# Linear attention and spectral mixing on one core: attention numerators of both head halves in one 128-row product

## The chip, the cores and the metric

The kernel runs on one core of a Trainium2 chip. The metric is the device time of one execution in microseconds, and lower is better. Data lie in HBM. SBUF is the on-chip memory with 128 partitions, and PSUM holds matmul results. TensorE (PE in the profile) multiplies; PEld is its loading of the stationary operand. VectorE (DVE), ScalarE (ACT), GpSimd (POOL) and SyncE (SP) are the other engines. Each engine works through its own instructions in order. POOL and SP here do little but issue DMA transfers, and POOL's transfers convert float32 in HBM to 16 bits in SBUF.

## The reference

There are two layers in a row. The first is linear attention over 8 batches, 8 heads, 576 rows and a head dimension of 64:

```python
def phi(x):
    return np.where(x > 0, x, np.exp(x) - 1.0) + 1.0
q_p, k_p = (phi(q), phi(k))
kv = np.einsum('bhsd,bhse->bhde', k_p, v)
z = np.sum(k_p, axis=2)
num = np.einsum('bhsd,bhde->bhse', q_p, kv)
den = np.einsum('bhsd,bhd->bhs', q_p, z)[..., None] + 1e-06
x = num / den
```

Its output, with the heads side by side, is x of 576 rows and 512 columns per batch. The second layer takes the real FFT along the rows, multiplies the first 64 modes with complex 512 x 512 matrices (one pair of matrices, `w_r` and `w_i`, per mode), leaves the other modes zero, transforms back to y, and gives `u + max(u @ w_ch, 0)` with `u = x + y`. The weights of the modes are 134 MB in float32, most of what the kernel reads.

## The kernel before

**Attention stage.** One loop runs over the 8 batches. `load` brings q, k and v of the batch two ahead, in two buffers each. `exps` (ACT) and `features` (DVE) form phi of q and k; `features` also copies v into `vpad`, which has one buffer and carries a column of ones, so that the sum z comes out of the same products as kv. In each turn of the loop the work is given in this order: `turn_q` transposes phi of q (PE, line 236) and copies it to SBUF (ACT, line 243); `sum_kv` sums kv of the batch (PE, line 256) and copies the parts that belong to one head to `kv_all` (ACT, line 268); `features` of the next batch; `exps` of the batch after next; then `form_x` five times, each for a set of rows. `form_x` multiplies transposed q with kv (`num_matmuls`, line 162), takes the reciprocal of the denominators (DVE, line 289) and multiplies (DVE, line 292) to get x in float16. Between these stand the forward DFT of the batch before (`transform`, line 354) and `place_x` (lines 322 to 343), which lays out the spectra of the batch before that for the mode products.

The order on each engine is written out by hand: `pin` keeps an instruction in program order. Three slots of PSUM (tag `big`) go round among the transposes, kv sums, numerators and spectra, in the order in which these are given.

A head pair fills the 128 partitions, so a batch has kv in four blocks of two 64-row halves. `num_matmuls` makes one matmul of 64 rows and 65 columns for each half (64 numerators and the denominator): eight per row set.

**Weights.** The modes go in pairs. The first five pairs are loaded during the attention stage, two into `wpool` and three into a pool that is given up afterwards. Every further pair reuses a buffer of `wpool`, so its load (POOL, line 116) waits until the product that used the buffer is done. On POOL's queue the loads of these first five pairs are followed by `wch16`, the channel weights (line 513), and `pick_sb` (line 515), and then by the sixth pair.

**Weight stage.** For each pair, `mode_pair` makes 16 matmuls (line 431), evacuates the result (lines 446 and 448), and transposes and sums it with `pick_sb` (line 454). Two slots per pair, "mid" and "end", take other work off a list: first `attention_rows`, which computes the numerators again for each of the 36 row tiles, this time as float32 rows of the final x (lines 162, 620 and 622); the constant row sets (`row_sets`, `row_set`), which stand after the eighth tile in the list; then the inverse DFT of the lower modes with the first channel products (lines 655 to 686), and the products that the last modes need. The denominators of even batches are kept from the attention stage, those of odd batches are taken again.

**Tail.** After the last weights have landed, the rest of the inverse DFT and of the channel product is added for pairs of row tiles (lines 737 to 810) and the rows are stored.

Of the kernel before, what the change touches and what calls it, by code (L numbers as in the profile page):

```python
# [10 lines left out]
F32 = mybir.dt.float32  # L11
F16 = mybir.dt.float16
# [31 lines left out]
def kernel(  # L44
# [10 lines left out]
    nc = tc.nc  # L55

    B, H, S, Dh = q.shape
    D = H * Dh
    NM = moe_w_r.shape[0]
    NHP = H // 2  # L60
    NDC = D // 128
# [15 lines left out]
    const = ctx.enter_context(tc.tile_pool(name="const", bufs=1, side="right"))  # L77
# [3 lines left out]
    id16 = const.tile([128, 128], F16, name="id16")  # L81
    fwd_sb = const.tile([128, 5, 2 * NM], F16, name="fwd_sb")
    pick_sb = const.tile([128, 32], F16, name="pick_sb")
    wch16 = const.tile([128, NDC, D], F16, name="wch16")
    actwarm = const.tile([128, 1], F32, name="actwarm")
    nc.vector.memset(actwarm, 0.0)
    nc.scalar.activation(out=actwarm, in_=actwarm, func=AF.Exp)
# [13 lines left out]
    kv_all = [xpool.tile([128, 2, 2, 65], F16, tag="kv", bufs=B, name=f"kv{b}") for b in range(B)]  # L101
    rd_all = [xpool.tile([128, 5, 2, 4], F32, tag="rd", bufs=B, name=f"rd{b}") for b in range(B)]

    W_KEEP = 2
    pin = tc.keep_in_program_order
    PIECES = (slice(0, 4), slice(4, 6), slice(6, 7), slice(7, 8))
    HALVES = [slice(0, 64), slice(64, 128)]
# [3 lines left out]
    def w_load(p: int, half: int, pool, tag: str, bufs: int):  # L111
        if half == 0:
            w_in[p] = pool.tile([128, NDW, D], BF16, tag=tag, bufs=bufs, name=f"w{p}")
        two = (moe_w_r, moe_w_i)[half][2 * p : 2 * p + 2]
        pin(
            nc.gpsimd.dma_start(  # L116
                out=w_in[p][half::2], in_=two.rearrange("g (r dc) e -> (g r) dc e", dc=NDW)
            )
        )
# [25 lines left out]
    def w_next():  # L145
        p, half = pending.pop(0)
        pool, tag, bufs = (wpool, "w", W_KEEP) if p < n_keep else (wpre, "wp", W_PRE)
        w_load(p, half, pool, tag, bufs)

    def rows_of(jj: int, base: int = 0):  # L150

        if jj < NJJ:
            return slice(base + jj, base + 512, NJJ)
        return slice(512, S) if base == 0 else slice(0, base)

    def num_matmuls(num, orow, qT, kv_sb, cols, pinned=False):
        for hpp in range(2):
            for h2 in range(2):
                for hpo in range(2):
                    rows = slice(hpo * 64, hpo * 64 + 64)  # L160
                    c0 = (hpp * 2 + h2) * 65
                    mm = nc.tensor.matmul(  # L162
                        num[hpo][orow, c0 : c0 + 65], qT[rows, hpp, h2, cols], kv_sb[rows, hpp, h2, :]
                    )
                    if pinned:
                        pin(mm)
        return [n[orow, 0:260].rearrange("p (c n) -> p c n", c=4) for n in num]

    def q_view(t):
        return t.rearrange("p (c t s) -> p c t s", c=2, t=2)  # L170

    qT_all = [q_tile(f"qT{b}") for b in range(B)]
# [75 lines left out]
    def sum_kv(b):  # L248

        for pair in range(2):  # L250
            kv_ps = psA.tile([128, 2, 512], F32, tag="big", bufs=3, name=f"kvp{b}_{pair}")
            for j in range(2 * NJ):
                for h2 in range(2):
                    r0 = 64 * pair + 32 * h2
                    pin(
                        nc.tensor.matmul(  # L256
                            kv_ps[:, h2, 0:130],
                            phi["k", b][r0 : r0 + 32, j // NJ, j % NJ].rearrange("p o d -> p (o d)"),
                            vp[r0 : r0 + 32, :, j, 0:65],
                            start=(j == 0),  # L260
                            stop=(j == 2 * NJ - 1),
                            tile_position=(r0, 0),
                        )
                    )
            for hpo in range(2):
                rows = HALVES[hpo]
                pin(
                    nc.scalar.copy(
                        out=kv_all[b][rows, pair], in_=kv_ps[rows, :, hpo * 65 : hpo * 65 + 65]
                    )  # L270
                )

    def form_x(b, jj):
        if jj == 0:
            x16s[b] = (
                sA.tile([128, 2 * NJ * Dh * 2], F16, tag="x16", bufs=2, name=f"x16_{b}")[
                    :, 0 : NJJ * D
                ].rearrange("p (j d) -> p j d", j=NJJ),
                sA.tile([128, D], F16, tag="x16t", bufs=2, name=f"x16t_{b}"),
            )  # L280
        tail = jj == NJJ
        orow = HALVES[b % 2] if tail else slice(0, 128)
        num = psA.tile([128, 2, 512], F32, tag="big", bufs=3, name=f"num{b}_{jj}")
        num_matmuls(
            [num[:, o] for o in range(2)], orow, q_view(qT_all[b]), kv_all[b], rows_of(jj), True
        )
        nv = num[orow, :, 0:260].rearrange("p o (c n) -> p o c n", c=4)
        rden = rd_all[b][orow, jj]
        pin(nc.vector.reciprocal(out=rden, in_=nv[:, :, :, 64]))
        dst = x16s[b][1][orow, :] if tail else x16s[b][0][:, jj, :]  # L290
        pin(
            nc.vector.tensor_tensor(  # L292
                out=dst.rearrange("p (o c d) -> p o c d", o=2, c=4),
                in0=nv[:, :, :, 0:64],
                in1=rden.unsqueeze(3).broadcast_to([64 if tail else 128, 2, 4, Dh]),
                op=ALU.mult,
            )
        )

    place = sA.tile([128, 4, 66], BF16, name="place")  # L300
    place_l = sA.tile([128, 2, 130], BF16, name="place_l")
    nc.vector.memset(place, 0.0)
    nc.vector.memset(place_l, 0.0)

# [204 lines left out]

    while pending:  # L510
        w_next()
    tc.keep_in_program_order(
        nc.gpsimd.dma_start(out=wch16, in_=moe_w_ch.rearrange("(c p) j -> p c j", p=128))
    )
# [34 lines left out]
    sW = ctx.enter_context(tc.tile_pool(name="sW", bufs=1))  # L549
# [8 lines left out]
    BASE = (0, 64)  # L558
    out_rows = out.rearrange("b s d -> (b s) d")

    def x_of(t: int):
        if t < B * NJJ:
            return x_main[t // NJJ][:, t % NJJ, :]
        i = t - B * NJJ
        return x_tail[i // 2][:, i % 2, :]
# [10 lines left out]
    def bank(name: str, shape=(128, D), dtype=F32):  # L576
        return psB.tile(list(shape), dtype, tag="bank", bufs=4, name=name)
# [25 lines left out]
    def parts_of(t: int):  # L603
        if t < B * NJJ:
            b, jj = divmod(t, NJJ)
            return [(b, jj, slice(0, 128))]
        p = t - B * NJJ
        return [(2 * p + h, NJJ, HALVES[h]) for h in range(2)]

    def attention_rows(t: int):  # L610

        num = [bank(f"nw{t}_{o}") for o in range(2)]
        x = x_of(t)
        for b, jj, orow in parts_of(t):
            nv = num_matmuls(num, orow, q_view(qT_all[b]), kv_all[b], rows_of(jj, BASE[b % 2]), True)
            for o in range(2):
                rden = rd_all[b][orow, jj, o]
                if b % 2 == 1:
                    rden = sW.tile([128, 4], F32, tag="rdw", bufs=4, name=f"rdw{t}_{o}")[orow]
                    pin(nc.vector.reciprocal(out=rden, in_=nv[o][:, :, 64]))  # L620
                pin(
                    nc.vector.tensor_tensor(  # L622
                        out=x[orow, o * 256 : o * 256 + 256].rearrange("p (c d) -> p c d", c=4),
                        in0=nv[o][:, :, 0:64],
                        in1=rden.unsqueeze(2).broadcast_to([orow.stop - orow.start, 4, Dh]),
                        op=ALU.mult,
                    )
                )

    def early_rows(b: int):  # L630

# [56 lines left out]
    tiles = []  # L688
# [63 lines left out]
    for b in range(B):  # L752
        pairs += [(b * NJJ, b * NJJ + 1), (b * NJJ + 2, b * NJJ + 3)]
        if b % 4 == 3:
            k = b // 4
# [90 lines left out]
    def share(n_items: int, steps: list):  # L846
        total, at = sum(w for _, w in steps), 0
        for key, w in steps:
            lo = at
            at += w  # L850
            slots[key] = slots.get(key, 0) + n_items * at // total - n_items * lo // total
# [13 lines left out]
    def first_rows(n: int):  # L865
# [7 lines left out]
            )  # L873

    rows_work = [row_sets] + [lambda i=i: row_set(i) for i in range(1 + N_LEAD)]
    work[:0] = [lambda t=t: attention_rows(t) for t in tiles[:8]] + rows_work + [
        lambda t=t: attention_rows(t) for t in tiles[8:]
    ]
    share(
        len(tiles) + len(rows_work),  # L880
        [((p, h), 1) for p in range(n_early, first_fold) for h in ("mid", "end")],
# [22 lines left out]
    rows = [Y8[:, ec].rearrange("p m n -> p (m n)") for ec in range(NDC)]  # L904
# [17 lines left out]
    for h, eng in enumerate((nc.sync, nc.gpsimd)):  # L922
        eng.dma_start(
            out=YZ_all[64 * h : 64 * h + 64 : NF // NL].rearrange("r b z d -> r b (z d)"),
            in_=last.rearrange("p z d -> p (z d)"),
# [10 lines left out]
    def add_one(n: int, i: int):  # L936
# [8 lines left out]
            out=x_of(0), in0=accs[0][:, 0], scalar=0.0, in1=x_of(0), op0=ALU.max, op1=ALU.add  # L945
# [51 lines left out]
```

## Time and profile before

| | |
|---|---|
| Median of 3 runs | 421.31 us (421.26 to 423.99) |
| Profiled execution | 421.64 us, span 419.9 us |
| PE busy | 289.4 us (69%) |
| PEld busy | 156.2 us (37%) |
| DVE busy | 228.3 us (54%) |
| ACT busy | 153.7 us (37%) |
| POOL busy | 57.0 us (14%) |
| Mean granted TensorE clock | 0.79 |
| HBM read, written | 163.9 MB, 9.4 MB |

The span is the time from the first to the last instruction in the profiler's record; the execution's own time has a little around it. Busy shares are averages over stages that differ: the attention stage (to about 113 us), the weight stage (to about 384 us) and the tail. In lines of the timeline the first two columns are the start and the duration in microseconds; then come the engine, the line of the kernel, the operation, its output and inputs with their shapes, how many instructions are merged, and in brackets the idle time of the engine just before, with what ended it. The granted clock of TensorE is a share of its full speed.

### The profile page before, as it was taken

What the parts mean: (1) busy time and instruction counts of PE and PEld (TensorE: products, weight loads), DVE (VectorE), ACT (ScalarE), POOL (GpSimd) and SP (SyncE); (2) the same over time, 40 slices, a digit from 0 to 9 for tenths busy, and PEclk for the clock granted to TensorE, in tenths of its full rate; (3) what the DMA queues carried; (4) which work ended last, traced back from release to release, by engine and by line L of the source; (5) the groups of instructions that cost most, each with busy time, mean ns of one, the idle gap of its engine ahead of it and who ended that gap; (6) DMA issues with size and microseconds to landing.
All of it is one profiled execution on the core that took longest, in us unless ns stands there. A gap on an engine that the chain in (4) does not pass through costs nothing.

```text
span 419.9 us, 7345 instructions
## 1 busy us (share of the span) xinstructions
PE 289.4 (69%) x3094; PEld 156.2 (37%) x3094; DVE 228.3 (54%) x495; ACT 153.7 (37%) x253; POOL 57.0 (14%) x99
## 2 busy tenths in 40 slices
PE   0359998999617553444343686979787978999992
PEld 0247776877301221222121232424333423364420
DVE  3588899695404462464645353455544533422794
ACT  4677797854201011000000233334342532230782
POOL 4222224210001111111111111101111111130000
PEclk9999988599855555555555589898998988899997
DMA  8999999999999999999999999999999999997698
GB/s 217 211 212 217 210 222 205 229 204 223 219 220 212 213 223 211 215 223 207 220 220 208 222 220 209 220 219 208 221 222 208 219 219 211 220 209 158 237 390 326
DMA packets 16417, 93.17 MB, mean 222 GB/s; under 512 B 2032, under 2 KB 2944, under 8 KB 11968
## 3 DMA queue, kind: packets, MB, share of 16 engines
q0 software_dynamic: 12416, 81.48, 93.2%
q1 hardware_dynamic: 3968, 11.22, 7.2%
q8 instruction: 24, 0.39, 0.3%
q14 instruction: 9, 0.07, 0.0%
HBM read 163.93 MB, written 9.44 MB: 413 GB/s over the span
## 4 chain that ended last, share of the span: by engine, by line
DMA 62%; PE 24%; DVE 5%; issue 3%; ACT 3%; POOL 2%; DVEq 0%; ACTq 0%; POOLq 0%
DMA w<-in_moe_w_i_dram 49%; DMA pick_sb<-row_pick 8%; PE P L431 8%; DMA k<-in_k_dram 5%; PE acc L737 3%; PE acc L776 2%; PE kvp L256 2%; PE zl L418 2%; POOL w L116 2%; PE eps L678 2%; ACT ke L207 1%; DVE x L292 1%; PE yt L454 1%; ACT ys L448 1%; DVE ke L220 1%
## 5 line engine op out<-in xcount | busy, mean ns | idle before, releaser
L431 PE MATMUL P<-w,xz 128*32 128x512 bf16 x496 | 49.4, 538 | 65.1 <-DMA w<-in_moe_w_i_dram 62.6
L448 ACT CAST ys<-P 128x512 f16<-128x512 f32 x15 | 8.8, 585 | 127.9 <-PE P L431 127.9
L116 POOL DMA_DIRECT2D w<-in_moe_w_r_dram x31 | 17.4, 560 | 246.3 <-PE P L431 241.8
L431 PEld LDWEIGHTS <-xz 128*32 128x32 bf16 x496 | 13.4, 116 | 86.8 <-DMA w<-in_moe_w_i_dram 55.4
L446 DVE CAST ys<-P 128x512 f16<-128x512 f32 x17 | 11.8, 692 | 56.8 <-PE P L431 56.8
L678 PE MATMUL eps<-wch,xTw 128*128 128x512 f16 x144 | 40.9, 412 | 0.0
L162 PEld LDWEIGHTS <-qT 64*128 64x128 f16 (+1 forms) x640 | 23.4, 124 | 31.3 <-issue 17.5
L661 ACT CAST x16w<-x_main 128x512 f16<-128x512 f32 x32 | 19.8, 618 | 37.0 <-DVE x_main L659 37.0
L659 DVE TENSOR_TENSOR x_main<-ya,x_main 128x512 f32<-128x512 f32 x32 | 22.0, 690 | 20.8 <-PE ya L655 20.5
L256 PE MATMUL kvp<-vpad,ke 32*128 32x130 f16 x576 | 24.6, 261 | 9.0 <-ACT qT L243 6.2
L686 ACT CAST E<-eps 128x512 f16<-128x512 f32 (+1 forms) x40 | 21.2, 539 | 22.6 <-PE eps L678 22.6
L441 DVE COPY xz<-xt_c 64x256 bf16<-64x256 bf16 x62 | 23.1, 372 | 11.2 <-PE P L431 10.4
L256 PEld LDWEIGHTS <-ke 32*128 32x128 f16 x576 | 22.4, 115 | 10.8 <-issue 8.3
L162 PE MATMUL nw<-kv,qT 64*128 64x65 f16 (+1 forms) x320 | 18.9, 240 | 9.5 <-DVE x_tail L622 4.5
L292 DVE TENSOR_TENSOR x<-num,rd 128x512 f16<-128x512 f32 x32 | 22.1, 691 | 1.1
L236 PE MATMUL qTp<-id,qe 128*128 128x128 f16 x144 | 13.3, 265 | 11.2 <-DVE qe L220 9.7
L207 ACT ACTIVATE qe<-q 128x1152 f16<-128x1152 f16 (+1 forms) x16 | 17.9, 1157 | 8.0 <-DMA q<-in_q_dram 7.9
L622 DVE TENSOR_TENSOR x_main<-nw,rd 128x256 f32<-128x256 f32 x32 | 11.2, 415 | 17.3 <-PE nw L162 17.3
L162 PE MATMUL num<-kv,qT 64*128 64x65 f16 (+1 forms) x320 | 16.6, 219 | 5.1 <-DVE x L292 2.4
L243 ACT COPY qT<-qTp 128x1152 f16<-128x1152 f16 x16 | 19.6, 1292 | 0.7 <-PE qTp L236 0.6
L454 PE MATMUL yt<-pick_sb,ys 128*128 128x32 f16 (+1 forms) x128 | 8.7, 185 | 16.0 <-DMA pick_sb<-row_pick 9.8
L207 ACT ACTIVATE ke<-k 128x1152 f16<-128x1152 f16 x16 | 17.7, 1154 | 5.3 <-DMA k<-in_k_dram 3.9
(117 smaller groups left out, 492.5 us busy)
## 6 DMA issues: line engine op xcount, KB each, us to landing
w<-in_moe_w_r_dram POOLq DMA_DIRECT2D x31, 1024.0 KB, 12.5
w<-in_moe_w_i_dram POOLq DMA_DIRECT2D x31, 1024.0 KB, 16.9
out_dram<-x_main SPq DMA_DIRECT2D x10, 512.0 KB, 4.7
k<-in_k_dram POOLq DMA_DIRECT2D x8, 576.0 KB, 12.9
v<-in_v_dram POOLq DMA_DIRECT2D x8, 576.0 KB, 14.4
q<-in_q_dram POOLq DMA_DIRECT2D x7, 576.0 KB, 12.6
out_dram<-x_main SPq DMA_DIRECT2D x2, 1024.0 KB, 4.9
q<-in_q_dram SPq DMA_DIRECT2D x2, 576.0 KB, 4.6
```

Source lines behind the costliest of these rows:

```text
L116: nc.gpsimd.dma_start(out=w_in[p][half::2], in_=two.rearrange("g (r dc) e -> (g r) dc e", dc=NDW))
L162: mm = nc.tensor.matmul(num[hpo][orow, c0 : c0 + 65], qT[rows, hpp, h2, cols], kv_sb[rows, hpp, h2, :])
L207: pin(nc.scalar.activation(out=ev[:, c], in_=heads(nm, b, c), func=AF.Exp))
L243: nc.scalar.copy(out=qT[:, :, c * NJ : (c + 1) * NJ], in_=qT_ps.rearrange("p j x -> p x j"))
L256: nc.tensor.matmul(kv_ps[:, h2, 0:130], phi["k", b][r0 : r0 + 32, j // NJ, j % NJ].rearrange("p o d -> p (o d)"), vp[r0 : r0 + 32, :, j, 0 ...
L292: nc.vector.tensor_tensor(out=dst.rearrange("p (o c d) -> p o c d", o=2, c=4), in0=nv[:, :, :, 0:64], in1=rden.unsqueeze(3).broadcast_to([ ...
L431: nc.tensor.matmul(P[c : c + n, :], x, w[:, dc, :], start=(dc < NDC), stop=(dc >= n_dc - NDC), tile_position=(0, c), skip_group_check=True,)
L441: pin(nc.vector.tensor_copy(out=xz[p % 2][HALVES[h], :, h, :], in_=src))
L659: pin(nc.vector.tensor_tensor(out=x, in0=acc, in1=x, op=ALU.add))
L661: pin(nc.scalar.copy(out=x16w[t], in_=x))
L678: nc.tensor.matmul(e_ps, xT[:, c, :], wch16[:, c, :], start=(c == 0), stop=(c == NDC - 1))
L686: pin(nc.scalar.copy(out=dst, in_=e_ps[:, cols]))
```

## The change

The two halves of a head pair become one matmul. Its moving operand is a block-diagonal kv: 128 rows and 2 x 65 columns, with the first head's kv in the upper rows and left columns, the second head's in the lower rows and right columns, and zeros elsewhere. A row set then takes four matmuls of 128 rows and 130 columns instead of eight of 64 rows and 65 columns, and its result lies in PSUM in a different order of columns.

In the attention stage the block-diagonal tile `bd_all` has space for two batches. It lies in the space that the channel weights take later: both have the tag `wch` with one buffer, so `wch16` is now allocated after the loop. `sum_kv` lets ACT copy into `bd_all`, and two new copies on VectorE at its end fill `kv_all` from it. In the weight stage a second such tile, `kv_diag_w`, is filled from `kv_all` by `set_kv`, one row tile ahead of its use. It takes the space (tag `rows`) in which the row sets' selector and later `ye_slots` lie, so the row sets now come after all attention rows.

```diff
-    wch16 = const.tile([128, NDC, D], F16, name="wch16")
+    bd_all = const.tile([128, NDC * D], F16, tag="wch", bufs=1, name="kv_diag")[:, 0 : 2 * 520]
+    bd_all = bd_all.rearrange("p (i a h n) -> p i a h n", i=2, a=2, h=2)
...
-    def num_matmuls(num, orow, qT, kv_sb, cols, pinned=False):
+    def num_matmuls(num, orow, qT, kv_bd, cols):
         for hpp in range(2):
             for h2 in range(2):
-                for hpo in range(2):
-                    rows = slice(hpo * 64, hpo * 64 + 64)
-                    c0 = (hpp * 2 + h2) * 65
-                    mm = nc.tensor.matmul(
-                        num[hpo][orow, c0 : c0 + 65], qT[rows, hpp, h2, cols], kv_sb[rows, hpp, h2, :]
-                    )
-                    if pinned:
-                        pin(mm)
-        return [n[orow, 0:260].rearrange("p (c n) -> p c n", c=4) for n in num]
+                c0 = h2 * 256
+                pin(nc.tensor.matmul(num[hpp][orow, c0 : c0 + 130], qT[:, hpp, h2, cols], kv_bd[:, hpp, h2]))
+
+    def diag_part(kv_bd, hpo: int):
+
+        return kv_bd[HALVES[hpo], :, :, hpo * 65 : hpo * 65 + 65]
...
                 pin(
                     nc.scalar.copy(
-                        out=kv_all[b][rows, pair], in_=kv_ps[rows, :, hpo * 65 : hpo * 65 + 65]
+                        out=diag_part(bd_all[:, b % 2], hpo)[:, pair],
+                        in_=kv_ps[rows, :, hpo * 65 : hpo * 65 + 65],
                     )
                 )
+        for hpo in range(2):
+            pin(nc.vector.tensor_copy(out=kv_all[b][HALVES[hpo]], in_=diag_part(bd_all[:, b % 2], hpo)))
...
+    nc.vector.memset(bd_all, 0.0)
     nc.vector.memset(place, 0.0)
...
     while pending:
         w_next()
+    wch16 = const.tile([128, NDC, D], F16, tag="wch", bufs=1, name="wch16")
     tc.keep_in_program_order(
         nc.gpsimd.dma_start(out=wch16, in_=moe_w_ch.rearrange("(c p) j -> p c j", p=128))
     )
...
+    bdw: list = []
+
+    def set_kv(b: int):
+
+        if not bdw:
+            bdw.append(sW.tile([128, 2, 2, 2, 130], F16, tag="rows", bufs=1, name="kv_diag_w"))
+            nc.vector.memset(bdw[0], 0.0)
+        for hpo in range(2):
+            pin(nc.vector.tensor_copy(out=diag_part(bdw[0][:, b % 2], hpo), in_=kv_all[b][HALVES[hpo]]))
...
+        k = tiles.index(t) + 1
+        for b in sorted({p[0] for t_next in tiles[k : k + 1] for p in parts_of(t_next)} - kv_set):
+            kv_set.add(b)
+            set_kv(b)
...
-    work[:0] = [lambda t=t: attention_rows(t) for t in tiles[:8]] + rows_work + [
-        lambda t=t: attention_rows(t) for t in tiles[8:]
-    ]
+    kv_set = {0}
+    set_kv(0)
+    work[:0] = [lambda t=t: attention_rows(t) for t in tiles] + rows_work
```

The rest of the diff follows from this: `form_x` and `attention_rows` read PSUM in its new order of columns, with as many DVE instructions of as many elements as before.

More of the change, by code (lines that the diff above doesn't have):

```diff
@@ L283, in form_x @@
         num = psA.tile([128, 2, 512], F32, tag="big", bufs=3, name=f"num{b}_{jj}")
[L284 to L288, printed above, removed]
+        num_matmuls([num[:, a] for a in range(2)], orow, q_view(qT_all[b]), bd_all[:, b % 2], rows_of(jj))
+        nv = num.rearrange("p a (h m) -> p (a h) m", h=2)[orow, :, 0:130]
+        nv = nv.rearrange("p c (o n) -> p c o n", o=2)
+        rden = rd_all[b][orow, jj].rearrange("p a (h o) -> p (a h) o", h=2)
         pin(nc.vector.reciprocal(out=rden, in_=nv[:, :, :, 64]))
@@ L292, in form_x @@
             nc.vector.tensor_tensor(
-                out=dst.rearrange("p (o c d) -> p o c d", o=2, c=4),
+                out=dst.rearrange("p (o c d) -> p c o d", o=2, c=4),
                 in0=nv[:, :, :, 0:64],
-                in1=rden.unsqueeze(3).broadcast_to([64 if tail else 128, 2, 4, Dh]),
+                in1=rden.unsqueeze(3).broadcast_to([64 if tail else 128, 4, 2, Dh]),
                 op=ALU.mult,
@@ L608, in parts_of @@
         return [(2 * p + h, NJJ, HALVES[h]) for h in range(2)]
+    bdw: list = []
[5 more added lines that the diff above has]
+            pin(nc.vector.tensor_copy(out=diag_part(bdw[0][:, b % 2], hpo), in_=kv_all[b][HALVES[hpo]]))
     def attention_rows(t: int):
-        num = [bank(f"nw{t}_{o}") for o in range(2)]
+        num = [bank(f"nw{t}_{a}") for a in range(2)]
         x = x_of(t)
         for b, jj, orow in parts_of(t):
-            nv = num_matmuls(num, orow, q_view(qT_all[b]), kv_all[b], rows_of(jj, BASE[b % 2]), True)
-            for o in range(2):
-                rden = rd_all[b][orow, jj, o]
+            num_matmuls(num, orow, q_view(qT_all[b]), bdw[0][:, b % 2], rows_of(jj, BASE[b % 2]))
+            for a in range(2):
+                nv = num[a].rearrange("p (h m) -> p h m", h=2)[orow, :, 0:130]
+                nv = nv.rearrange("p h (o n) -> p h o n", o=2)
+                rden = rd_all[b][orow, jj, a].rearrange("p (h o) -> p h o", h=2)
                 if b % 2 == 1:
-                    rden = sW.tile([128, 4], F32, tag="rdw", bufs=4, name=f"rdw{t}_{o}")[orow]
-                    pin(nc.vector.reciprocal(out=rden, in_=nv[o][:, :, 64]))
+                    rden = sW.tile([128, 2, 2], F32, tag="rdw", bufs=4, name=f"rdw{t}_{a}")[orow]
+                    pin(nc.vector.reciprocal(out=rden, in_=nv[:, :, :, 64]))
+                xv = x[orow, :].rearrange("p (o a h d) -> p a h o d", o=2, a=2, h=2)[:, a]
                 pin(
                     nc.vector.tensor_tensor(
-                        out=x[orow, o * 256 : o * 256 + 256].rearrange("p (c d) -> p c d", c=4),
-                        in0=nv[o][:, :, 0:64],
-                        in1=rden.unsqueeze(2).broadcast_to([orow.stop - orow.start, 4, Dh]),
+                        out=xv,
+                        in0=nv[:, :, :, 0:64],
+                        in1=rden.unsqueeze(3).broadcast_to([orow.stop - orow.start, 2, 2, Dh]),
                         op=ALU.mult,
```

## The prediction

> **What bounds the kernel now.** I read the page first: the slices, then the chain that ended last.
>
> ```profile
> span 419.9 us, 7345 instructions
> ...
> DMA  8999999999999999999999999999999999997698
> ...
> DMA 62%; PE 24%; DVE 5%; issue 3%; ACT 3%; POOL 2%; DVEq 0%; ACTq 0%; POOLq 0%
> DMA w<-in_moe_w_i_dram 49%; DMA pick_sb<-row_pick 8%; PE P L431 8%; DMA k<-in_k_dram 5%; PE acc L737 3%; PE acc L776 2%; PE kvp L256 2%; PE zl L418 2%; POOL w L116 2%; PE eps L678 2%; ACT ke L207 1%; DVE x L292 1%; PE yt L454 1%; ACT ys L448 1%; DVE ke L220 1%
> ```
>
> The DMA engines are busy from the first slice to the 36th. Two thirds of the chain are transfers, nearly all of mode weights. From 124.7 us to 384 us the kernel is a stream of weight pairs at one per 9.7 us (two pairs per 19.4 us in the chain), then about 35 us of tail. So the end moves only if this stream starts later, or gets a hole. I therefore looked for what starts it: the timeline of POOL, then of PE, around the end of the attention stage.
>
> ```profile
> 86.98 0.77 POOL L513 DMA_DIRECT2D wch<-in_moe_w_ch_dram  x1 [4.09 <-DMA w<-in_moe_w_r_dram]
> 91.82 0.54 POOL L515 DMA_DIRECT2D pick_sb<-row_pick  x1 [4.07 <-DMA w<-in_moe_w_i_dram]
> 115.27 0.52 POOL L116 DMA_DIRECT2D w<-in_moe_w_r_dram  x1 [22.91 <-PE P L431]
> ```
>
> ```profile
> 113.06 1.90 PE L431 MATMUL P<-w,xz 128*32 128x512 bf16 x16 [2.45 <-issue]
> 124.75 0.27 PE L454 MATMUL yt<-pick_sb,ys 128*128 128x32 f16 x4 [9.79 <-DMA pick_sb<-row_pick]
> ```
>
> [...]The first load that needs a used buffer, the sixth pair's, is issued at 115.27, when the first mode product is done (114.96). The queue at that time still holds work until 124.7 (pick_sb, its last entry, has just landed). So there is a **cushion**: the sixth pair starts moving at about 124.9, where 115.3 plus some 1.7 us to start (an estimate: 0.52 us of issue on POOL and about 1 us to the first byte on this path, by the specifications in the Trainium skill's "DMA: Bandwidth & Descriptors") would have sufficed. Up to 124.9 - 117.0 = 7.9 us of delay in the attention stage costs nothing; every microsecond beyond moves the end one for one.
>
> What sets the attention stage is VectorE. One batch, on VectorE, then ACT, then PE:
>
> ```profile
> 51.72 0.68 DVE L292 TENSOR_TENSOR x16t<-num,rd 64x512 f16<-64x512 f32 x1
> 52.33 0.74 DVE L214 TENSOR_SCALAR q<-q 128x2304 f16<-128x2304 f16 x1
> ...
> 56.58 0.75 DVE L226 COPY vpad<-v 128x2304 f16<-128x2304 f16 x1
> 57.25 0.20 DVE L289 RECIPROCAL rd<-num 128x8 f32<-128x8 f32 x1
> ```
>
> ```profile
> 55.35 1.14 ACT L268 CAST kv<-kvp 64x130 f16<-64x130 f32 x4
> ```
>
> ```profile
> 52.17 1.18 PE L236 MATMUL qTp<-id,qe 128*128 128x128 f16 x18
> 53.28 2.31 PE L256 MATMUL kvp<-vpad,ke 32*128 32x130 f16 x72
> ```
>
> The last division of batch 2 is followed at once by the feature work of batch 4 (52.33), and that runs **beside** batch 3's transposes and kv sums on PE and kv copies on ACT, which end at 56.49. VectorE has no gap here: its own work per batch is 4.25 us (features) + 0.67 (vpad) + 5.10 (numerators, 57.25 to 62.35) = 10.0 us.
>
> The same PE work earlier, and ACT's copies after it:
>
> ```profile
> 40.20 2.10 PE L236 MATMUL qTp<-id,qe 128*128 128x128 f16 x18
> 42.23 3.63 PE L256 MATMUL kvp<-vpad,ke 32*128 32x130 f16 x72
> ```
>
> ```profile
> 45.91 0.55 ACT L268 CAST kv<-kvp 64x130 f16<-64x130 f32 x2 [0.95 <-PE kvp L256]
> ```
>
> The granted clock was half in this stretch and until about 50 us: from the first transpose to the last kv copy 6.26 us, against 4.32 us at full clock (52.17 to 56.49).
>
> **What the Trainium skill says.** "PSUM — Partial Sum Buffer", section "Engine vs sequencer instructions": ScalarE, VectorE and GpSimdE queues are strict FIFO. The trace agrees: vpad at 45.91 waited 0.92 us for PE and all after it waited too. "TensorE: Matmul & The Clock Gate", section on the HAM clock gate: half clock is the default, and an idle window of some 3.4 us brings it back. The trace agrees on the price (2.31 against 3.63 us for the same 72 matmuls). "DMA: Bandwidth & Descriptors", "Anatomy of one DMA": waits sit on the issuing sequencer, the DMA engines just drain their queues. This is the cushion, 115.3 to 124.7.
>
> **The change, part by part.**
>
> *The added copies.* After each batch's kv copies on ACT, two pinned copies on VectorE (diagonal part to kv_all, 64 x 260 f16) stand ahead of the next batch's features in VectorE's order. They wait for ACT's kv copies, which wait for PE's kv sums. Behind them queue features, vpad, numerators; for features wait the next transposes on PE, for the q, k, v buffers the loads on POOL. So the 4.25 us of features no longer lie beside PE's sums but after them. The copies' own price: nothing of this shape in the trace; the 128x64 copy (0.20 us) and the strided 64x256 one (0.37 us) bound it, and the skill's "VectorE: DVE Perf Modes", errata section, gives an estimate of 58 cycles plus 260, at 0.96 GHz 0.33 us, less in a fast mode. I take 0.27, two are 0.55 us.
>
> Could PE run further ahead to close this gap? The numerators, transposes and sums share three PSUM slots, and the slot of the first kv sum is that of the fifth numerator, free at the end T of the batch's divisions. At half clock PE also has three numerators (0.45 us each, 4 x 130 columns at the transposes' 117 ns for 128) and four DFT groups (0.77) after the first division frees a slot, 4.4 us, while VectorE needs 4.05: transposes start at T + 0.3.
>
> - Half clock: kv copies end at T + 0.3 + 6.2 = T + 6.5, copies T + 7.1, plus 10.0: a batch takes 17.1 us.
> - Full clock: PE chain 2.9 us, so transposes are over by T; sums to T + 2.4; ACT (xsp 0.97, qT 2.46, kv 1.14) to T + 3.45; copies T + 4.0; plus 10.0: 14.0 us.
>
> Before, starts of feature work were 29.42, 40.63, 52.33, 62.35, 72.21, 85.96 us: about 10 to 11.7, and once 13.7. Now step by step, at half clock. Batch 0: kv copies at 24.3 (unchanged, ACT timeline), copies, features and vpad to 29.8, numerators with the place copies to 34.7 (before: 29.4). Batch 1: transposes at 33.0 once the third division frees their slot, sums to 38.7, copies to 39.8, numerators (no cast of xp, 4.2) to 48.9. Batch 2: 65.6 (+16.7). Batches 3 to 6: 82.7, 99.8, 116.9, 134.0. Batch 7 has no features ahead: 6.5 + 0.6, then PE-paced numerators, 13.7: 147.7. From there to the first product's end 10.0 us before (105.0 to 114.96, mostly full clock), 12.5 at half: 160. At full clock from batch 2 on: 62.9, 76.9, 90.9, 104.9, 118.9, then 9.0 and 10: 137.9.
>
> The sixth pair's load is then issued at 160.3 or 138.2 instead of 115.3, starts 1.7 us later at 162.0 or 139.9, against 124.9: **+37 or +15 us**. The queue is empty by then: v of batch 7 is asked for at about 95 (half clock), with 16.8 MB of weights behind it, 39 us at 9.7 us per 4.2 MB. Nothing later can give it back, since the stream runs at its own rate and PE's later work is beside it.
>
> *Block-diagonal matmuls.* 320 pairs of load and matmul become 160 in each stage. No gain in time: the two row halves ran side by side (8 matmuls of 65 columns in 0.34 us, 37.17 to 37.51, at half clock). I cost them at +0.1 us per tile in the attention stage, counted above. In the weight stage they lie beside 9.7 us of transfer per pair; if that cover were gone, 32 tiles by 0.1 us, 3 us.
>
> *kv_diag_w.* One memset and 16 copies, some 4.6 us of VectorE in the weight stage, which is a third busy: nothing. Uncovered: 4.6 us.
>
> *wch later.* Its load waits for batch 7's numerators; pick_sb and the sixth pair queue behind it on POOL. Numerators end 10 us before the first product does, so pick_sb is ahead of need, and the sixth pair waits for the product anyway: nothing. Alone it would move wch from 87 to 105, still ahead of 115.
>
> *bd_all memset, row sets last.* VectorE is idle to 6.1 us; the row sets keep the number of work slots: nothing. Uncovered, under 1 us and about 3 us (three matmul pairs, six ACT copies).
>
> **Rivals.**
> 1. *Full clock.* PE is dense in 14 of 17 us, and full clock came in after some 10 us of dense work at 50.2 and 84.3. Against: each time the window before held xp, numerators and DFT groups without a gap; now PE idles 3 us after xp, while VectorE does features. It gives 421.6 + 15 = 437.
> 2. *The cushion absorbs it* (not slower). Features' wait would have to cost under 7.9 us in seven batches, about 1.1 each, that is kv sums would have to end near T. For: PE is only 69% busy. Against: the PSUM slot, and 3.45 us at best. It gives 421.6.
> 3. *The product doesn't get cheaper or the copies are cheap*: neither decides, as the wait is three to six microseconds and the copies 0.55; at 0.2 or 0.37 a copy, 1.1 less or 1.6 more over eight batches.
>
> **The numbers.** The profiled execution took 421.64 us (span 419.9, 1.7 around it); the median of the runs is 421.31, which I treat as the same. Likeliest: half clock except in two of the batches, 421.6 + 37 - 2 x 3.1 = **453 us**, chance 62% (446 to 460). Rival 1 and mixtures near it, 434 to 446: 27%. Rival 2: 4%. Above 460: 5%. A gain over 1%: 2%. Range **435 to 460**. Within 1% (about what this kernel's measurement can tell from no change): 4%; slower by more: 94%.
>
> **What would show it.** Right: idle time of VectorE before the two copies, released by ACT's kv copies, 3.5 to 6.5 us in each of batches 1 to 6; feature work starting 14 to 17 us apart; slices of DMA below 9 in the first 150 us; the sixth pair's load after 135 us; pairs 9.7 us apart afterwards and the same tail. Wrong if feature work still starts 10 us apart, or if the load's issue comes before 123 us.

## The result and the profile after

The changed kernel takes 457.64 us (median of 6 runs, 455.56 to 459.88), the kernel before 421.82 us in the same comparison. The ratio is 1.084, with a 95% interval of 1.0795 to 1.0885. The profiled execution took 455.56 us (span 453.1 us), 33.9 us more than the profiled one of before (421.64 us).

First the page of the changed kernel: span, slices of DMA, shares of the chain.

```profile
span 453.1 us, 6747 instructions
...
DMA  8999697499994499999999999999999999999598
...
DMA 49%; PE 32%; DVE 10%; issue 4%; POOL 2%; ACT 2%; DVEq 0%; ACTq 0%; POOLq 0%
```

The row of DMA, which before was at 9 from the second slice to the 36th, has holes in two places: in the 5th, 7th and 8th slice and in the 13th and 14th (a slice is now 11.3 us). The first hole lies in the attention stage, the second at its end, before the sixth pair's load. The chain has given up transfers for PE and VectorE. From the 15th slice to the 36th the row is as before.

Now the waits of the changed kernel (who waited for whom: total, times, longest), and VectorE's timeline around batch 3:

```profile
DVE kv L272 <- ACT kv_diag L266: 49.1, 8, 9.2
...
PE num L161 <- DVE x L292: 29.3, 8, 5.0
```

```profile
61.83 0.68 DVE L292 TENSOR_TENSOR x16t<-num,rd 64x512 f16<-64x512 f32 x1
69.10 0.56 DVE L272 COPY kv<-kv_diag 64x260 f16<-64x260 f16 x2 [6.59 <-ACT kv_diag L266]
69.69 0.76 DVE L212 TENSOR_SCALAR q<-q 128x2304 f16<-128x2304 f16 x1
...
73.97 0.75 DVE L224 COPY vpad<-v 128x2304 f16<-128x2304 f16 x1
74.64 0.20 DVE L289 RECIPROCAL rd<-num 128x8 f32<-128x8 f32 x1
```

Where feature work followed the last division at once (51.72 and 52.33 before), there are now 6.59 us of idle time until ACT's kv copies. The copies themselves are cheap. The second wait is the mirror image: PE stands while VectorE does the features it could not do earlier. PE and VectorE take turns.

PE in the same stretch, and the granted clock in two stretches of the windows (columns: window and length, busy time and instructions of PE, PEld, DVE, ACT and POOL, clock, DMA share, GB/s):

```profile
63.04 2.10 PE L234 MATMUL qTp<-id,qe 128*128 128x128 f16 x18
65.07 3.63 PE L254 MATMUL kvp<-vpad,ke 32*128 32x130 f16 x72
```

```profile
60.00:65.00 5.00, 5.00 (x41) 3.76 (x38) 2.39 (x6) 2.17 (x4) 0.00 (x0) 0.50 1.11 211
...
85.00:90.00 5.00, 1.97 (x32) 1.47 (x30) 4.53 (x8) 4.86 (x6) 0.72 (x1) 1.00 0.00 0
```

The transposes begin 0.5 us after the division ends at 62.5, at half clock (0.50 in the first line). The second line shows DMA at zero, with VectorE and ACT busy.

Last, POOL and PE at the end of the stage:

```profile
142.84 0.77 POOL L515 DMA_DIRECT2D wch<-in_moe_w_ch_dram  x1 [41.74 <-DVE x L292]
143.60 0.55 POOL L517 DMA_DIRECT2D pick_sb<-row_pick  x1
153.95 0.52 POOL L117 DMA_DIRECT2D w<-in_moe_w_r_dram  x1 [9.80 <-PE P L432]
```

```profile
151.84 1.81 PE L432 MATMUL P<-w,xz 128*32 128x512 bf16 x16 [2.45 <-issue]
154.44 0.29 PE L455 MATMUL yt<-pick_sb,ys 128*128 128x32 f16 x4 [0.79 <-DVE ys L447]
```

The sixth pair's load is issued at 153.95 instead of 115.27, 38.7 us later. pick_sb no longer holds anything up: PE waits 0.79 us for VectorE where it waited 9.79 us for pick_sb. The last product of the weights (the one that ends the stream), before and after:

```profile
386.94 1.50 PE L502 MATMUL y_last<-xt_c,w 128*128 128x16 bf16 x32
```

```profile
420.42 1.07 PE L503 MATMUL y_last<-xt_c,w 128*128 128x16 bf16 x32
```

It starts 33.5 us later, and the tail is as long as before (32.7 us to the end of the span, 33.0 before).

### The profile page after: what moved, and what is told of

Same layout as the page of the kernel before. It is cut to its first block, busy times and chain, and to the rows that moved or that the text cites. A ratio compares the mean times of both kernels' runs of the same rounds, so it can differ in the third digit from the quotient of the medians.

```text
span 453.1 us, 6747 instructions
## 1 busy us (share of the span) xinstructions
PE 308.3 (68%) x2774; PEld 170.1 (38%) x2774; DVE 236.1 (52%) x529; ACT 154.8 (34%) x253; POOL 56.2 (12%) x99
## 4 chain that ended last, share of the span: by engine, by line
DMA 49%; PE 32%; DVE 10%; issue 4%; POOL 2%; ACT 2%; DVEq 0%; ACTq 0%; POOLq 0%
DMA w<-in_moe_w_i_dram 44%; PE P L432 5%; PE kvp L254 5%; DMA k<-in_k_dram 3%; PE qTp L234 3%; PE xf L355 3%; PE num L161 3%; DVE qe L218 2%; PE z L719 2%; PE acc L756 2%; PE zl L419 2%; PE acc L795 2%; POOL w L117 1%; DVE x L292 1%; PE xf L360 1%
## 5 line engine op out<-in xcount | busy, mean ns | idle before, releaser
L432 PE MATMUL P<-w,xz 128*32 128x512 bf16 x496 | 48.5, 531 | 62.5 <-DMA w<-in_moe_w_i_dram 60.0
L161 PEld LDWEIGHTS <-qT 128*128 128x128 f16 (+1 forms) x320 | 29.1, 137 | 62.7 <-DVE x L292 30.5
L161 PE MATMUL num<-kv_diag,qT 128*128 128x130 f16 (+1 forms) x160 | 22.8, 293 | 32.4 <-DVE x L292 29.3
L697 PE MATMUL eps<-wch,xTw 128*128 128x512 f16 x144 | 39.8, 403 | 0.0
L161 PE MATMUL nw<-kv_diag_w,qT 128*128 128x130 f16 (+1 forms) x160 | 24.2, 301 | 12.0 <-DVE kv_diag_w L620 6.2
L254 PE MATMUL kvp<-vpad,ke 32*128 32x130 f16 x576 | 26.3, 281 | 7.4 <-ACT qT L241 4.6
L272 DVE COPY kv<-kv_diag 64x260 f16<-64x260 f16 x16 | 3.6, 225 | 49.7 <-ACT kv_diag L266 49.1
L254 PEld LDWEIGHTS <-ke 32*128 32x128 f16 x576 | 24.3, 126 | 9.2 <-issue 7.5
L234 PE MATMUL qTp<-id,qe 128*128 128x128 f16 x144 | 17.0, 312 | 9.7 <-DVE qe L218 9.4
L689 DVE COPY xTw<-xTp 128x512 f16<-128x512 f16 x36 | 15.0, 417 | 9.1 <-PE xTp L687 9.1
L419 PE MATMUL zl<-wch,id 128*128 128x512 f16 x72 | 19.4, 405 | 0.0
```

The lines of the kernel that those rows point to most:

```text
L161: pin(nc.tensor.matmul(num[hpp][orow, c0 : c0 + 130], qT[:, hpp, h2, cols], kv_bd[:, hpp, h2]))
L234: nc.tensor.transpose(qT_ps[:, j], phi["q", b][:, c, j].rearrange("p o d -> p (o d)"), id16,)
L254: nc.tensor.matmul(kv_ps[:, h2, 0:130], phi["k", b][r0 : r0 + 32, j // NJ, j % NJ].rearrange("p o d -> p (o d)"), vp[r0 : r0 + 32, :, j, 0 ...
L419: pin(nc.tensor.matmul(last_ps[0], id16, wch16[:, 0, :]))
L432: nc.tensor.matmul(P[c : c + n, :], x, w[:, dc, :], start=(dc < NDC), stop=(dc >= n_dc - NDC), tile_position=(0, c), skip_group_check=True,)
L697: nc.tensor.matmul(e_ps, xT[:, c, :], wch16[:, c, :], start=(c == 0), stop=(c == NDC - 1))
```

## The experiments

The theory: the two copies on VectorE make the features wait for kv, the attention stage grows, and past a cushion the weight stream starts that much later. Its rivals: the products of another form, the shared space of `wch`, or the weight stage's part costs the time; or the clock does not matter.

**The copies behind the features.** All of the change stays; the copies become a function of their own, called behind the features.

```diff
+
+    def keep_kv(b):
         for hpo in range(2):
             pin(nc.vector.tensor_copy(out=kv_all[b][HALVES[hpo]], in_=diag_part(bd_all[:, b % 2], hpo)))
...
         if b + 1 < B:
             for _ in features(b + 1):
                 pass
+        keep_kv(b)
```

> The changed kernel with one edit: the two copies to kv_all on VectorE stand behind the next batch's features instead of ahead of them. Block-diagonal products, the shared space of wch and everything in the weight stage stay. The wait theory: the features lie beside PE's sums again, VectorE pays only 16 copies of 0.23 us (3.6 us, under the cushion of 7.9 us), the sixth pair's load comes before 120 us, time 420 to 424. The rival that the products, the shared wch space or the weight stage cost the time: 450 or more.

Measured: 421.42 us, ratio to the kernel before 0.998 (0.996 to 1.000). Its timelines of VectorE and POOL:

```profile
75.11 0.74 DVE L212 TENSOR_SCALAR q<-q 128x2304 f16<-128x2304 f16 x1
...
80.03 0.48 DVE L274 COPY kv<-kv_diag 64x260 f16<-64x260 f16 x2
85.59 0.76 DVE L212 TENSOR_SCALAR q<-q 128x2304 f16<-128x2304 f16 x1
...
90.53 0.48 DVE L274 COPY kv<-kv_diag 64x260 f16<-64x260 f16 x2
```

```profile
103.91 0.77 POOL L518 DMA_DIRECT2D wch<-in_moe_w_ch_dram  x1 [21.45 <-PE num L161]
104.66 0.55 POOL L520 DMA_DIRECT2D pick_sb<-row_pick  x1
115.41 0.52 POOL L117 DMA_DIRECT2D w<-in_moe_w_r_dram  x1 [10.21 <-PE P L435]
```

In these batches the same copies now wait for nothing, and feature work is 10.5 us apart (75.11 and 85.59). Only in batch 7, which has no features ahead, do they still wait (3.64 us). The sixth pair's load is back at 115.41, although `wch` still waits 21 us on POOL. So the products, the shared space and the weight stage together cost nothing that can be measured in this order (time within 0.4% of before); the place of two copies costs it all.

**The wait alone in the kernel before.**

```diff
                         out=kv_all[b][rows, pair], in_=kv_ps[rows, :, hpo * 65 : hpo * 65 + 65]
                     )
                 )
+        for hpo in range(2):
+            pin(nc.vector.tensor_copy(out=actwarm[HALVES[hpo]], in_=kv_all[b][HALVES[hpo], 1, 1, 64:65]))
```

> The kernel before with one addition: after each batch's kv copies two pinned copies of 64 x 1 elements of kv on VectorE, ahead of the next batch's features; nothing reads them. Matmuls, wch and the weight stage stay as before. The wait theory: VectorE stands 4 to 6.6 us per batch, the sixth pair's load comes at 140 to 155, time 445 to 458. The rival (products, wch, weight stage): 421 to 424, since tiny copies cost under 3 us in all.

Measured: 453.62 us, ratio 1.073 (1.067 to 1.080). The profile of this kernel:

```profile
86.93 0.44 DVE L273 CAST actwarm<-kv 64x1 f32<-64x1 f16 x2 [5.99 <-ACT kv L268]
87.40 0.76 DVE L214 TENSOR_SCALAR q<-q 128x2304 f16<-128x2304 f16 x1
```

```profile
107.43 0.77 POOL L515 DMA_DIRECT2D wch<-in_moe_w_ch_dram  x1 [4.28 <-DMA w<-in_moe_w_r_dram]
...
153.88 0.52 POOL L116 DMA_DIRECT2D w<-in_moe_w_r_dram  x1 [41.06 <-PE P L433]
```

Two copies of one column, with no other part of the change, move the load to 153.88, next to the 153.95 of the changed kernel. The effect is made by the wait and not by the copies' work.

The medians still differ by 4 us (453.6 and 457.6), but the two profiled executions don't: both have a span of 453.1 us. So the traces can't show where the 4 us come from, and it stays open. They do show a small difference within a batch, in stretches where the matmuls are equally slow:

```profile
82.96 3.63 PE L256 MATMUL kvp<-vpad,ke 32*128 32x130 f16 x72
```

These are the same 3.63 us as in the changed kernel at 65.07. Feature work is 16.4 us apart here (70.99 to 87.40) and 17.2 in the changed kernel (85.85 to 103.04). The chain of three numerators and four DFT groups before the transposes takes 4.0 us here (76.91 to 80.92) and 4.5 us there (75.62 to 80.15); the first group of numerators is 0.34 us long here and 0.42 us there. In the two profiles the changed kernel makes this good: its matmuls are fast again from about 141.5 us on, here they stay slow to about 147.

**Filling TensorE's idle time.** The changed kernel with more work for PE:

```diff
     def transform(b, dc):
-        if dc == 0:
+        if b not in xfs:
...
+    FILL_A = 14
...
+            if b > 0 and jj == 1:
+                xfs[b - 1] = psA.tile([128, NDC, 2, NM], F32, tag="xf", bufs=2, name=f"xf{b - 1}")
+                for _ in range(FILL_A):
+                    pin(
+                        nc.tensor.matmul(
+                            xfs[b - 1].rearrange("p c t m -> p (c t m)"), id16,
+                            fwd_sb[:, 0:4, :].rearrange("p j n -> p (j n)"),
+                        )
+                    )
```

> The changed kernel with 14 matmuls of 128 x 512 on TensorE after each batch's second numerator (batches 1 to 7), into the PSUM tile of the transform, overwritten later. They fill the time in which TensorE waits for VectorE's features, so that the granted clock stays full. If half the clock is what makes a batch 17 us instead of 14: batches at 14 to 14.5 us from batch 3 on, time 437 to 445. If the clock matters little: 455 to 460; if the fill delays the numerators, above 460.

Measured: 442.31 us, ratio 1.047 (1.042 to 1.051), 15.3 us less than without the 98 extra matmuls. PE, VectorE and POOL in this kernel:

```profile
63.73 2.31 PE L254 MATMUL kvp<-vpad,ke 32*128 32x130 f16 x72
...
68.64 3.18 PE L400 MATMUL xf<-fwd_sb,id 128*128 128x512 f16 x14
73.13 0.43 PE L161 MATMUL num<-kv_diag,qT 128*128 128x130 f16 x4 [1.31 <-DVE x L292]
...
125.65 3.18 PE L400 MATMUL xf<-fwd_sb,id 128*128 128x512 f16 x14
128.66 0.40 PE L161 MATMUL num<-kv_diag,qT 128*128 128x130 f16 x4
```

```profile
95.60 0.52 DVE L272 COPY kv<-kv_diag 64x260 f16<-64x260 f16 x2 [3.63 <-ACT kv_diag L266]
...
109.58 0.52 DVE L272 COPY kv<-kv_diag 64x260 f16<-64x260 f16 x2 [3.48 <-ACT kv_diag L266]
```

```profile
141.65 0.52 POOL L117 DMA_DIRECT2D w<-in_moe_w_r_dram  x1 [9.46 <-PE P L442]
```

Up to batch 6 the fill lies almost wholly in time that PE spent waiting. In batch 7, which has no features ahead, it lies in the way: the numerators start at 128.66, when the fill's 3.0 us are over. The sums run in 2.31 us instead of 3.63, VectorE's wait in batches 2 to 7 is 3.5 to 4.3 us where it was 4.4 to 6.6, and the batches shown are 14.0 us apart (95.60 to 109.58; from batch 1 on the distances are 13.4 to 14.8). So of the change's 35.8 us some 15 come back when PE's idle time is filled: they are the half clock that the wait itself brought about. The other 20 us are the wait proper, with the fill's own cost in batch 7 and the few stretches that were still slow.

**One, two and three waits.** As in the first experiment, but in some batches the copies stay ahead of the features: in batch 3; in 2 and 5; in 2, 4 and 6.

```diff
+        if b in (2, 5):
+            keep_kv(b)
...
         if b + 1 < B:
             for _ in features(b + 1):
                 pass
+        if b not in (2, 5):
+            keep_kv(b)
```

> As the kernel with the late copies, but in batch 3 alone the two copies stand ahead of the next features. The wait then costs once, some 4 to 6.5 us, and with the copies' 3.6 us the attention stage ends 7.6 to 10 us later than before. If the cushion of 7.9 us is there: 421 to 424. If every delay reaches the end: 429 to 432.

> As the kernel with one wait, but in batches 2 and 5 the copies stand ahead of the next features. Each wait is taken as the 6.3 us that one wait moved the sixth pair's load (121.7 against 115.4): load at 128, that is 4.8 us beyond the cushion's edge (124.9 less 1.7 us), time 425 to 429. If there were no cushion: 434. If waits overlap with other gaps and do not add up: 421 to 423.

> The same with batches 2, 4 and 6. Load at 134.3, 11.1 us beyond the edge, time 430 to 436. If there were no cushion: 440. If waits do not add up: under 427.

Measured: 422.31 us, ratio 1.001 (0.999 to 1.003); 429.69 us, 1.018 (1.012 to 1.024); 435.56 us, 1.033 (1.030 to 1.037). The POOL line of the sixth pair in each of the three:

```profile
121.72 0.52 POOL L117 DMA_DIRECT2D w<-in_moe_w_r_dram  x1 [9.59 <-PE P L438]
```

```profile
128.96 0.52 POOL L117 DMA_DIRECT2D w<-in_moe_w_r_dram  x1 [10.01 <-PE P L438]
```

```profile
133.36 0.52 POOL L117 DMA_DIRECT2D w<-in_moe_w_r_dram  x1 [10.21 <-PE P L438]
```

One, two and three waits move the load by 6.45, 13.7 and 18.1 us from 115.27, that is 6.0 to 6.8 us for each, so they add up (they stand in different batches, so the steps need not be equal). One wait doesn't reach the end by more than the measurement shows; two and three do. The two waits ended 0.7 us above what was expected: the load came at 129.0, not 128, and the cushion was smaller than I had taken. From the ninth pair on the stream is steady. The ninth pair's load before, with one wait, and in the changed kernel:

```profile
146.45 0.54 POOL L116 DMA_DIRECT2D w<-in_moe_w_r_dram  x1 [6.65 <-PE P L431]
```

```profile
147.77 0.54 POOL L117 DMA_DIRECT2D w<-in_moe_w_r_dram  x1 [6.41 <-PE P L438]
```

```profile
179.27 0.54 POOL L117 DMA_DIRECT2D w<-in_moe_w_r_dram  x1 [9.07 <-PE P L432]
```

How much later it is than before shows how much of the delay was swallowed:

| kernel | sixth pair's load, later by | ninth pair's load, later by | swallowed |
|---|---|---|---|
| one wait | 6.45 us | 1.32 us | 5.13 us |
| two waits | 13.69 us | 7.90 us | 5.79 us |
| three waits | 18.09 us | 12.70 us | 5.39 us |
| changed, with fill | 26.38 us | 20.90 us | 5.48 us |
| wait alone | 38.61 us | 32.91 us | 5.70 us |
| changed | 38.68 us | 32.82 us | 5.86 us |

The cushion is there, at 5.1 to 5.9 us. In the profile of the three waits (438.08 us, above the median) two of the last pairs' loads came 11.9 and 14.6 us apart instead of 9.7 (362.5, 374.4, 389.0), which is a loss of its own late in the stream. PE was busy 9.48 of 10 us from 375 to 385 us there, at a granted clock of 0.50, so the product that the last of these loads waited for seems to have stood behind slow work on PE. No run tests this alone.

## Why the prediction was right

- **The stream of weights sets the end.** Right: the delay at the ninth pair's load, 32.8 us, is close to the delay at the stream's last product, 33.5, and in the span, 33.2.
- **The copies put the features behind kv.** Right, and it is the whole effect, by the first two experiments. VectorE's idle time before the copies was 3.4 to 6.6 us in batches 1 to 6, where 3.5 to 6.5 had been worked out; feature work came 13.8, 14.3, 17.2, 16.2, 17.2 and 17.1 us apart, against 14.0 at full and 17.1 at half clock.
- **Half clock in all but two batches.** Right in sum, and the closeness of the sum is luck: it gave a load at 160.3 - 6.2 = 154.1, and it came at 153.95. The 6.2 us were not saved by two batches of 14 us. Against the working at half clock the last divisions of batches 1 and 2 ended 1.4 and 3.1 us early, those of batch 7 4.0 us early, and another 2.4 us came after them, where the way to the first product took 10.0 us and not 12.5. The rival of full clock was priced at 437; the fill, with full clock in most of the stage, took 442.
- **How half clock was read.** The prediction says that the granted clock was half before until about 50 us. The profile's record of the granted clock reads 1.00 from 40 to 50 us; it is the lengths of the matmuls that are those of half clock (3.63 us for 72 sums at 42.23, as in the changed kernel at 65.07, where the record reads 0.50). The argument rests on the lengths and stands.
- **The cushion of 7.9 us.** The mechanism was right, the size was not: it measured 5.1 to 5.9. The mis-sized term is the 1.7 us from the issue until the pair moves on an empty queue (its two parts, 0.52 and about 1 us, make only 1.5). In the changed kernel the pair issued at 153.95 and 154.47 landed 12.39 us after the second issue, at 166.86, so 12.9 us after the first; if 9.7 of these are its bytes at the stream's rate, its start took 3.2. That explains 1.5 of the missing 2.0 to 2.8 us; the rest is open.
- **453 and the measured time.** The prediction's own sum gives 452.4. The profiled execution took 455.56, 3.2 us more: 2.0 are the cushion's, 0.4 come between the ninth pair's load and the end, and 0.7 lie outside the span (2.5 us there, 1.7 before). The median lies 2 us above that profile, which was the fastest of the six executions. No other has a trace, and their mean granted clocks (0.744 to 0.849, the profiled one 0.739) don't point to a slower clock; why they took longer stays open.
- **The copies' price.** Taken at 0.27 us, measured 0.226 (the median of the 16). It decides nothing, as was said.
- **Nothing gained by the block-diagonal products.** Right: with the copies out of the way the time is the same within 0.4%, and a group of numerators is longer at half clock (0.42 against 0.34 us, both from start to start; 0.45 was taken).
- **wch later, kv_diag_w, row sets: nothing.** Right, by the first experiment, which has all three.
- **The rival of the cushion** fell: it holds for one wait, not for seven.

## What to carry to other kernels

An instruction that is cheap by itself is priced by what it waits for and by what stands behind it in its engine's order: here 0.5 us of copies per batch, placed one step too early, made two engines take turns. Where a step only keeps a result for later, put it behind the work that doesn't need it. And where a queue of transfers sets the end, read how much work it still holds when the next load is issued: so much delay is free, less what an empty queue takes to start (here the queue held 9.6 us of work, and 5.1 to 5.9 us of delay were free).

## What the runs showed of the hardware that I had not expected

- Adding 98 matmuls that compute nothing of use saved 15.3 us (457.64 to 442.31). They filled most of PE's waits for VectorE, and the matmuls after them were fast (72 sums in 2.31 us instead of 3.63).
- Half clock lasts through dense work. In the changed kernel PE was busy 5.00 of 5.00 us from 60 to 65 us and 4.59 of 5.00 in the next 5, and the granted clock stayed at 0.50 in both windows.
- The record of the granted clock can disagree with the lengths of the matmuls. With the wait alone it reads 1.00 from 40 to 100 us, yet the 72 sums at 82.96 take 3.63 us.
- The first weight pair on an empty queue took 12.9 us from issue to landing, 3.2 us more than its 9.7 us in the stream.
